# A second feed-forward stage by Strassen's seven products, in 256-token chunks, with ScalarE's mish and memory handed over by stage

## The chip, the cores and the metric

The kernel runs on one core of a Trainium2 chip. The metric is device time in microseconds of one execution. The engines are TensorE (PE; its weight loads appear as PEld), VectorE (DVE), ScalarE (ACT), GpSimd (POOL) and SyncE (SP), which issues all DMAs of this kernel.

## The reference

Attention with a memory term over 4 batches of 576 tokens, then two feed-forward stages over all 2304 tokens. The change is in the last one, `_moe2_ref`:

```
x = attention(q, k, v, M_prev, z_prev, beta)     # 2304 x 512
a = x @ w1; b = x @ w2; x = (a * b @ w3) @ w_out # first stage, 512 -> 1024 -> 512
h = x @ w_in                                     # second stage, 512 -> 2048
sp = where(h > 20, h, log1p(exp(min(h, 20))))
g = h * tanh(sp)                                 # mish
return g @ w_out                                 # 2048 -> 512
```

The weights come as float64. `conv` reads each as two 32-bit words and makes a float32 of it.

## The kernel before

The kernel records its operations and orders them itself. `Recorder.op` notes an operation with its engine, its estimated cost and the buffers that it reads and writes; `schedule` then simulates the engines with these costs and writes the instructions in the order that comes out. TensorE's operations keep nearly the order in which they were recorded (their key is their number plus a bias); the other engines take what is most urgent. A buffer is a tag with a fixed number of copies (`BUFS`), so an operation also waits until an older copy of its tag is free. Each engine executes its instructions strictly in the order written.

Products are made of float32 operands split into a high part (a cast to the format fp32r) and a low part (the rest): `HL` gives three matmuls, high x high, high x low and low x high, where one would do in lower precision. All matmuls are issued at line 331 (`mm`), whatever their stage.

The program has three parts. Attention (heads of `SC`, `SE`, `AV`) and the first feed-forward stage (`ffn1`, `ffn1o`) are interleaved; the first stage writes its result, transposed, to a DRAM tensor `x2d`. The last units of the first stage run alone after attention has ended. Then comes the second stage:

- `load_ffn2(m)` loads two 128-row weight blocks (512 KB each) and splits them into high and low parts. They go into memory that earlier parts have done with, by the list `HOMES` (tags V, QK, e0, ld, PH of attention; wE, wB, wD, wA of the first stage's weights; Rr, mnl). The raw data pass through three buffers (`RAWS`: Rr and two of mnl). Some of these loads are recorded among the last first-stage units (`F2N`).
- The tokens are cut into five chunks (`CH`: three of 512, two of 384). `load_x2` reads a chunk from `x2d` and splits it.
- `h_blk(c, m)`, for each of 16 blocks of 128 hidden features: 12 matmuls as wide as the chunk (4 parts of the model dimension x 3), then mish by hand: Exp, two VectorE operations, Ln, Exp, two VectorE multiplications, and the split of the result into `gh` and `gl`.
- `fin(c, m, ...)`, four blocks later (`LA`=4): for each 128-token part of the chunk three matmuls 512 wide, accumulated over the 16 blocks in a PSUM bank of its own.
- At the chunk's end ScalarE copies each bank out, and SyncE writes it.

PSUM has eight banks (tag g) for everything. The accumulators of a 512 chunk take four.

Of the kernel before, what the change touches and what calls it, by code (L numbers as in the profile page):

```python
# [14 lines left out]
P = 128  # L15
NEG = -8.0e9
E20 = 485165195.40979028
# [55 lines left out]
class Recorder:  # L73
# [9 lines left out]
    def op(self, eng, cost, fn, r=(), w=()):  # L83
# [26 lines left out]
        return o  # L110

# [152 lines left out]
def kernel(  # L264
# [40 lines left out]
    const = ctx.enter_context(tc.tile_pool(name="const", bufs=1))  # L305
    wp = ctx.enter_context(tc.tile_pool(name="wp", bufs=1))
    sp_ = ctx.enter_context(tc.tile_pool(name="sp", bufs=1))
# [19 lines left out]
    def dma(dst, src, nbytes, r=(), w=()):  # L327
        op("sp", max(500, nbytes / 340.0), lambda: nc.sync.dma_start(out=dst(), in_=src()), r, w)
# [20 lines left out]

    mask = const.tile([P, P], BF16, name="mask")  # L350
# [4 lines left out]
    two = const.tile([P, 1], F32, name="two")  # L355
# [7 lines left out]
    nc.vector.memset(two, 2.0)  # L363
# [310 lines left out]
    def conv(src, rawb, c=None, part=None):  # L674
# [9 lines left out]
        act(512, cv, lambda: hw().bitcast(F32), [(raw, 1)], [ck], False, AF.Prelu, scale=2.0 ** -111, alpha=-(2.0 ** 32))  # L684
# [13 lines left out]
    def wcol(t, h, kk):  # L698
        return t.tile[:, h].rearrange("p (k f) -> p k f", k=KD)[:, kk, :]
# [89 lines left out]
    wi, wt = {}, {}  # L789
    HOMES = ["V", "QK", "QK", "e0", "ld", "PH"] + ["wE"] * 4 + ["wB"] * 8 + ["wD"] * 4 + ["wA"] * 8 + ["Rr", "mnl"]  # L790
    RAWS = ("Rr", "mnl", "mnl")

    def load_ffn2(m):
        for n, dst, src in ((2 * m, wi, moe2_w_in), (2 * m + 1, wt, moe2_w_out)):
            load_w(dst, src, m, HOMES[n], lambda n=n: buf(RAWS[n % 3 if n < 30 else 2], [P, 512, 2], I32))

    CH = [(sum(CFG["CH"][:x]), n) for x, n in enumerate(CFG["CH"])]
    xc = {}

    def load_x2(c):  # L800
        t0, n = CH[c]
        need = [x for x in range(2 * B) if x * HS < t0 + n and (x + 1) * HS > t0]
        xc[c] = []
        for kk in range(KD):
            raw = buf(("vr", "pl")[kk % 2], [P, 512])
            dma(lambda kk=kk, raw=raw: raw.tile[:, 0:n], lambda kk=kk: x2d[kk * P:(kk + 1) * P, t0:t0 + n], 512 * n,
                r=[(fx2[x], 2 * (kk // 2) + 1) for x in need], w=[raw])
            xx = buf("u", [P, 2, 512], F32R)
            act(n, lambda raw=raw, xx=xx: xx.tile[:, 0, 0:n], lambda raw=raw: raw.tile[:, 0:n], [raw], [(xx, 0)])
            lo(n, lambda raw=raw, xx=xx: xx.tile[:, 1, 0:n], lambda raw=raw: raw.tile[:, 0:n], lambda xx=xx: xx.tile[:, 0, 0:n], [raw, (xx, 0)], [(xx, 1)])  # L810
            xc[c].append(xx)

    def h_blk(c, m):
        n = CH[c][1]
        ps = gbuf()
        for kk in range(KD):
            def f(kk=kk):
                for y, (wx, x) in enumerate(HL):
                    mm(ps.tile[:, 0:n], wcol(wi[m], wx, kk), xc[c][kk].tile[:, x, 0:n], kk == y == 0, kk == KD - 1 and y == 2)

            op("pe", 3 * t_mm(n), f, r=[(wi[m], 0), (wi[m], 1), (xc[c][kk], 0), (xc[c][kk], 1)], w=[ps])
        hv = lambda: ps.tile[:, 0:n]
        ub_ = buf("x", [P, 512])
        wb = buf("x", [P, 512])
        gh = buf("x", [P, 512], F32R)
        gl = buf("t", [P, 512], F32R)
        u = lambda: ub_.tile[:, 0:n]
        w_ = lambda: wb.tile[:, 0:n]
        act(n, u, hv, [ps], [ub_], True, AF.Exp, scale=2.0 ** -8)
        op("dve", t_dve(n, True), lambda: nc.vector.tensor_scalar(out=w_(), in0=u(), scalar1=E20, scalar2=2.0, op0=ALU.min, op1=ALU.add), r=[ub_], w=[wb])  # L830
        op("dve", t_dve(n), lambda: nc.vector.scalar_tensor_tensor(out=u(), in0=u(), scalar=E20, in1=w_(), op0=ALU.min, op1=ALU.mult), r=[ub_, wb], w=[ub_])  # L831
        act(n, w_, u, [ub_], [wb], False, AF.Ln, bias=two)
        act(n, w_, w_, [wb], [wb], False, AF.Exp, scale=-1.0)
        op("dve", t_dve(n), lambda: nc.vector.scalar_tensor_tensor(out=u(), in0=hv(), scalar=2.0 ** -8, in1=u(), op0=ALU.mult, op1=ALU.mult), r=[ps, ub_], w=[ub_])  # L834
# [5 lines left out]
    def fin(c, m, gt, acc):  # L840
        gh, gl = gt
        for t in range(CH[c][1] // P):
            ts_ = slice(t * P, (t + 1) * P)

            def f(ts_=ts_, t=t):
                o = acc[t][1]()
                mm(o, gh.tile[:, ts_], wt[m].tile[:, 0], m == 0, False)
                mm(o, gh.tile[:, ts_], wt[m].tile[:, 1], False, False)
                mm(o, gl.tile[:, ts_], wt[m].tile[:, 0], False, m == M2 - 1)

            op("pe", 3 * t_mm(512), f, r=[gh, gl, (wt[m], 0), (wt[m], 1)], w=[acc[t][0]])
# [113 lines left out]
    m2 = 0  # L965
    for n, u in enumerate(units[ui:]):
        u()
        if n >= CFG["F2N"][0] and n % CFG["F2N"][1] == 0 and m2 < CFG["F2N"][2]:
            load_ffn2(m2)
            m2 += 1  # L970
    load_x2(0)
    for m in range(m2, M2):
        load_ffn2(m)
    for c in range(len(CH)):
        t0, n = CH[c]
        acc = []
# [71 lines left out]
```

## Time and profile before

| | |
|---|---|
| median of 3 runs | 963.48 us (961.24 to 964.03) |
| the profiled execution | 963.81 us, its span 962.0 us |
| PE busy | 942.1 us (98%), 5440 matmul records |
| VectorE busy | 727.4 us (76%) |
| ScalarE busy | 607.4 us (63%) |
| GpSimd busy | 84.1 us (9%) |
| granted clock of PE | 0.996 of full over the span |
| chain that ended last | PE 73%, VectorE 14%, ScalarE 5%, DMA 3% |

The span runs from the first instruction of the program to its last; what lies around it is the 1.8 us between the two numbers. Times in the rows below count from the span's start. A matmul's end is modelled in these profiles, so the distance from one start to the next is what tells its cost.

### The profile page before, as it was taken

Reading aid. Unit: us, or ns where it says so; the run is one execution under the profiler, and the core shown is the slowest. Engines: PE = TensorE matmul, PEld = TensorE weight load, DVE = VectorE, ACT = ScalarE, POOL = GpSimd, SP = SyncE. Lnnn points to the kernel's source line nnn. Section 1 sums busy time; section 2 is a strip of 40 time slices with the busy share of each in tenths; the row PEclk is TensorE's granted clock in tenths of the full one; section 3 lists DMA queues with packets and bytes.
Section 4 is the critical chain, followed back from the end, with each engine's and each line's share of the span. In section 5 each row is a group of like instructions: output and inputs, shape, how many; then the busy total and the mean of one; then the engine's idle time right before and its main releaser. Section 6 shows DMA issues by size and latency. Waiting matters only on the chain.

```text
span 962.0 us, 15244 instructions
## 1 busy us (share of the span) xinstructions
PE 942.1 (98%) x5440; PEld 816.2 (85%) x5440; DVE 727.4 (76%) x1643; ACT 607.4 (63%) x1240; POOL 84.1 (9%) x70
## 2 busy tenths in 40 slices
PE   6999999999999999999999999999999999999998
PEld 3555888889899999999999988888888888998997
DVE  8999998899998889977573888537564756565663
ACT  6677776888787868766454676446454545554653
POOL 2111012312121102111000000000000000000000
PEclk9999999999999999999999999999999999999999
DMA  9779546434333424212572740020002000100000
GB/s 353 235 249 303 191 145 173 145 105 143 111 91 107 133 69 120 70 39 51 138 249 82 219 159 1 1 88 0 1 1 83 1 1 25 53 1 17 34 1 33
DMA packets 48316, 96.62 MB, mean 100 GB/s; under 512 B 11024, under 2 KB 23344, under 8 KB 48240
## 3 DMA queue, kind: packets, MB, share of 16 engines
q1 hardware_dynamic: 48240, 95.64, 31.9%
q8 instruction: 43, 0.70, 0.3%
q14 instruction: 33, 0.27, 0.1%
HBM read 85.85 MB, written 9.77 MB: 99 GB/s over the span
## 4 chain that ended last, share of the span: by engine, by line
PE 73%; DVE 14%; ACT 5%; DMA 3%; issue 3%; SPq 0%; POOL 0%; DVEq 0%; ACTq 0%; POOLq 0%
PE g L331 73%; DVE QK L334 2%; DVE t L348 2%; DVE e L348 1%; DVE mnl L348 1%; DVE t L687 1%; ACT t L340 1%; DVE wD L687 1%; DVE u L334 1%; DMA wA<-in_moe_w_out_dram 1%; ACT QK L338 1%; DVE g L561 1%; DMA vr<-x2d 1%; DVE u L685 1%; DVE e L334 1%
## 5 line engine op out<-in xcount | busy, mean ns | idle before, releaser
L331 PE MATMUL g<-u,wA 128*128 128x288 f32 (+2 forms) x1008 | 164.1, 315 | 1.5 <-DVE e L348 0.8
L331 PEld LDWEIGHTS g<-u,wA 128*128 128x128 f32 x1008 | 147.6, 188 | 10.1 <-DVE e L348 1.0
L348 DVE TENSOR_TENSOR t<-g,t 128x288 f32<-128x288 f32 (+6 forms) x344 | 121.8, 383 | 17.0 <-PE g L331 9.2
L581 POOL PARTITION_ALL_REDUCE t<-t x64 | 83.5, 1311 | 365.9 <-DVE t L348 323.1
L331 PE MATMUL g<-x,wB 128*128 128x288 f32 x768 | 111.7, 298 | 0.0
L331 PEld LDWEIGHTS g<-x,wB 128*128 128x128 f32 x768 | 105.0, 188 | 0.9 <-DVE e L348 0.2
L340 ACT ACTIVATE x<-x,two 128x512 f32<-128x512 f32 (+1 forms) x80 | 54.3, 681 | 68.0 <-DVE x L831 68.0
L340 ACT ACTIVATE x<-g 128x512 f32<-128x512 f32 (+1 forms) x98 | 54.7, 561 | 61.8 <-PE g L331 60.4
L331 PE MATMUL g<-e,V 128*65 128x320 f32 (+12 forms) x576 | 89.8, 302 | 1.8 <-DVE e L334 0.8
L331 PE MATMUL g<-QK 128*128 128x320 f32 (+7 forms) x464 | 77.1, 305 | 6.7 <-DVE QK L334 5.8
L834 DVE SCALAR_TENSOR_TENSOR x<-g,x 128x512 f32<-128x512 f32 (+1 forms) x80 | 50.9, 637 | 42.2 <-ACT x L340 41.8
L331 PEld LDWEIGHTS g<-e,V 128*65 128x65 f32 (+1 forms) x576 | 66.8, 137 | 18.6 <-ACT e L340 2.1
L338 ACT CAST x<-x 128x512 fp32r<-128x512 f32 (+1 forms) x80 | 46.1, 577 | 52.6 <-DVE x L348 52.5
L331 PEld LDWEIGHTS g<-QK 128*128 128x128 f32 x464 | 66.8, 196 | 14.6 <-DVE QK L334 8.0
L830 DVE TENSOR_SCALAR x<-x 128x512 f32<-128x512 f32 (+1 forms) x80 | 31.7, 398 | 59.7 <-ACT x L340 58.0
L334 DVE TENSOR_TENSOR t<-x 128x512 fp32r<-128x512 f32 (+1 forms) x80 | 50.9, 637 | 32.3 <-ACT x L338 31.1
L331 PE MATMUL g<-wB,wD 128*128 128x512 f32 x128 | 61.1, 617 | 3.7 <-DVE wD L687 2.1
L334 DVE TENSOR_TENSOR QK<-ld,QK 64x640 fp32r<-64x640 f32 (+1 forms) x80 | 59.7, 747 | 3.7 <-ACT QK L338 2.4
L331 PE MATMUL g<-x,wD 128*128 128x288 f32 x384 | 56.9, 297 | 0.3 <-DVE e L348 0.3
L331 PE MATMUL g<-x,wE 128*128 128x288 f32 x384 | 55.1, 299 | 0.6 <-ACT mnl L338 0.6
L348 DVE TENSOR_TENSOR x<-x 128x512 f32<-128x512 f32 (+1 forms) x80 | 51.0, 638 | 6.1
L831 DVE SCALAR_TENSOR_TENSOR x<-x 128x512 f32<-128x512 f32 (+1 forms) x80 | 50.9, 637 | 4.6
(147 smaller groups left out, 1810.1 us busy)
## 6 DMA issues: line engine op xcount, KB each, us to landing
ld<-in_qk_dram SPq DMA_DIRECT2D x24, 608.0 KB
u<-in_moe_w_dram SPq DMA_DIRECT2D x26, 512.0 KB
Rr<-d SPq DMA_DIRECT2D x24, 288.0 KB
mnl<-in_moe_w_out_dram SPq DMA_DIRECT2D x11, 512.0 KB
mnl<-in_moe_w_in_dram SPq DMA_DIRECT2D x11, 512.0 KB
x2d<-t SPq DMA_DIRECT2D x16, 288.0 KB
out_dram<-x SPq DMA_DIRECT2D x18, 256.0 KB
wA<-in_moe_w_out_dram SPq DMA_DIRECT2D x8, 512.0 KB
```

Of the source, the lines that this page charges most:

```text
L331: nc.tensor.matmul(out=o, lhsT=lhsT, rhs=rhs, start=start, stop=stop)
L334: eng.tensor_tensor(out=o, in0=a, in1=b, op=ALU.subtract)
L338: op("act", t_act(n, psum), lambda: nc.scalar.copy(out=o(), in_=i()), r, w)
L340: op("act", t_act(n, psum), lambda: nc.scalar.activation(out=o(), in_=i(), func=func, **kw), r, w)
L348: op(eng, t_dve(n) if eng == "dve" else t_pool(n), lambda: e.tensor_tensor(out=o(), in0=a(), in1=b(), op=alu), r, w)
L561: nc.vector.tensor_tensor(out=o, in0=o, in1=mv, op=ALU.add)
L581: op("pool", 430 + 2.6 * (b - a), lambda mv=mv: nc.gpsimd.partition_all_reduce(mv(), mv(), P, bass_isa.ReduceOp.max), r=[(m, x)], w=[(m, x)])
L685: op("dve", t_dve(512, True), lambda: nc.vector.tensor_scalar(out=lw(), in0=lw(), scalar1=29, scalar2=None, op0=ALU.logical_shift_right), ...
L687: op("dve", t_dve(512), lambda: nc.vector.scalar_tensor_tensor(out=ci(), in0=ci(), scalar=3, in1=lw(), op0=ALU.logical_shift_left, op1=ALU ...
L830: op("dve", t_dve(n, True), lambda: nc.vector.tensor_scalar(out=w_(), in0=u(), scalar1=E20, scalar2=2.0, op0=ALU.min, op1=ALU.add), r=[ub_ ...
L831: op("dve", t_dve(n), lambda: nc.vector.scalar_tensor_tensor(out=u(), in0=u(), scalar=E20, in1=w_(), op0=ALU.min, op1=ALU.mult), r=[ub_, w ...
L834: op("dve", t_dve(n), lambda: nc.vector.scalar_tensor_tensor(out=u(), in0=hv(), scalar=2.0 ** -8, in1=u(), op0=ALU.mult, op1=ALU.mult), r= ...
```

## The change

The second stage is written anew, and the memory around it.

- **Chunks** are 256 tokens (nine of them). The hidden features are taken in eight pairs of 128-blocks. `h_blk` makes both blocks of a pair in the two halves of one PSUM bank: 24 matmuls 256 wide.
- **Mish** is one ScalarE activation over the 512 columns of that bank (`AF.Mish`). It needs another table of functions; a recorded entry `table` puts its load after all uses of the old one.
- **The output product** treats two 128-token halves by two 128-feature halves as a 2 x 2 matrix, the output weights (two feature halves by two halves of 256 output columns) likewise, and multiplies them by Strassen's method (Winograd's form): seven products where there were eight. `g_blk` makes the sums on the token side for each pair (VectorE: operations of 128, 256 and 128 columns), then the split over 7 x 128 = 896 columns. `combine` makes the sums on the weight side, once, in chunk 0: four subtractions of 256 columns and splits of 1024 and 768. `fin` multiplies: seven products of three matmuls, 256 wide, each added into one of seven PSUM half-banks (`PRODUCTS`). `out_blk` puts the output together from them, by one ScalarE and four VectorE operations, and two writes of 256 KB.
- **Look-ahead** is two pairs (`LA`=2, before four blocks).
- **Memory** is handed over by stage. Two stacks of pools (`Room`): A1 holds what attention uses and becomes A2 (converted weights f, raw buffers s) when attention has ended; R1 holds what the first stage uses (x, u, t) and becomes R2 (G, H, ob, m) when that has ended. A tile of the new room waits for the tiles of the old one that lay where it lies. All 32 weight loads are therefore recorded after attention, through four raw buffers. Three pairs of input weights are loaded only when splits of earlier ones have given up their f buffers.

The diff, cut to its core:

```diff
+class Room:
+    def open(self):
+        if self.before is not None:
+            self.before.pool.release()
+        self.pool = self.tc.alloc_tile_pool(name=self.name, bufs=1, side=self.side, reuse_waits="tile")
...
+    def follow(self, room):
+        room.gate = o = self.op("pool", 0.0, room.open)
+        o.after = {x for x in self.ops if any(b.pool is room.before for b in x.bufs)}
...
+        "f": 13, "s": 4, "G": 2, "H": 2, "ob": 1, "m": 11, **CFG.get("BUFS", {}),
+    R1, A1 = Room(tc, "r1", "left"), Room(tc, "a1", "right")
+    R2, A2 = Room(tc, "r2", "left", R1), Room(tc, "a2", "right", A1)
...
+    def combine(i):
+        c, m = LC[i], buf("ob", [P, 3, 256])
+        for o, a, b in ((lambda: quarter(m, 0), lambda: quarter(c, 1), lambda: quarter(c, 3)),
+                        (lambda: quarter(c, 1), lambda: quarter(c, 1), lambda: quarter(c, 0)),
+                        (lambda: quarter(m, 1), lambda: quarter(c, 3), lambda: quarter(c, 1)),
+                        (lambda: quarter(m, 2), lambda: quarter(c, 2), lambda: quarter(m, 1))):
+            tt(256, o, a, b, ALU.subtract, [c, m], [c, m])
...
     def h_blk(c, m):
-        act(n, u, hv, [ps], [ub_], True, AF.Exp, scale=2.0 ** -8)
...
-        act(n, w_, u, [ub_], [wb], False, AF.Ln, bias=two)
-        act(n, w_, w_, [wb], [wb], False, AF.Exp, scale=-1.0)
...
+                            mm(ps.tile[:, y * CT:(y + 1) * CT], w[a].tile[:, y, kk * P:(kk + 1) * P], xc[c][j].tile[:, b, k * CT:(k + 1) * CT],
...
+    def g_blk(ps):
+        op("act", t_act(512, True), lambda: nc.scalar.activation(out=G.tile[:, 0:4].rearrange("p a b -> p (a b)"), in_=ps.tile, func=AF.Mish, scale=2.0 ** -8),
+           [ps, table], [(G, 0)])
+        tt(P, lambda: g(4), lambda: g(0), lambda: g(2), ALU.add, [(G, 0)], [(G, 1)])
+        tt(2 * P, lambda: G.tile[:, 5:7], lambda: G.tile[:, 0:5:4], lambda: g(1).unsqueeze(1).to_broadcast([P, 2, P]), ALU.subtract, [(G, 0), (G, 1)], [(G, 1)])
+        tt(P, lambda: g(7), lambda: g(3), lambda: g(6), ALU.subtract, [(G, 0), (G, 1)], [(G, 1)])
+        act(7 * P, lambda: H.tile[:, 0], g7, [(G, 0), (G, 1)], [(H, 0)])
+        lo(7 * P, lambda: H.tile[:, 1], g7, lambda: H.tile[:, 0], [(G, 0), (G, 1), (H, 0)], [(H, 1)])
...
+    PRODUCTS = [(0, 0, 0, 3, 0), (2, 0, 2, 0, 1), (5, 1, 1, 0, 0), (3, 0, 1, 1, 1), (4, 1, 0, 1, 0), (6, 0, 3, 2, 1), (1, 1, 2, 2, 0)]
+    def fin(c, i, H, acc):
+        for n, (k, d, qd, bank, half) in enumerate(PRODUCTS):
...
+                mm(o, gh, quarter(U, qd), i == 0 and first, False)
+                mm(o, gh, quarter(L, qd), False, False)
+                mm(o, gl, quarter(U, qd), False, i == NP2 - 1 and last)
...
+    rec.follow(A2)
+    loads = [(LC, moe2_w_out, i, y) for i in range(NP2) for y in range(2)]
+    loads += [(WC, moe2_w_in, i, y) for i in range(5) for y in range(2)]
     for n, u in enumerate(units[ui:]):
         u()
+        if n >= CFG["F2N"] and loads:
+            conv2(*loads.pop(0))
+    rec.follow(R2)
+    for i in range(NP2):
+        split_in(i)
+        if i < 3:
+            for y in range(2):
+                conv2(WC, moe2_w_in, i + 5, y)
+    op("act", 1400, lambda: None, w=[table])
+    load_x2(0)
+    for c in range(NC):
+        acc = [gbuf() for _ in range(4)]
...
+                if c == 0:
+                    combine(i)
+                ps = h_blk(c, i)
+            if i >= LA:
+                fin(c, i - LA, gts.pop(i - LA), acc)
+            if i < NP2:
+                gts[i] = g_blk(ps)
+            if i == NP2 - 1 and c + 1 < NC:
+                load_x2(c + 1)
+        out_blk(c, acc)
```

What this makes of the order of the instructions shows at three places. First TensorE, at the end of the first stage (the 96 matmuls of `ffn1o` with wA) and the begin of the second. Before:

```order
L331 MATMUL g<-u,wA 128x288 x96
L331 MATMUL g<-u,V 128x512 x3
L331 MATMUL g<-u,QK 128x512 x3
L331 MATMUL g<-u,V 128x512 x3
L331 MATMUL g<-u,QK 128x512 x3
L331 MATMUL g<-u,ld 128x512 x6
L331 MATMUL g<-u,wE 128x512 x9
```

And in the change (s is the chunk's data, wE and wB input weights; the rows with H are the output products, with weights of wA, f and m):

```order
L357 MATMUL g<-u,wA 128x288 x96
L357 MATMUL g<-s,wE 128x256 x48
L357 MATMUL g<-s,wB 128x256 x42
L357 MATMUL g<-wA,H 128x256
L357 MATMUL g<-f,H 128x256
L357 MATMUL g<-wA,H 128x256 x2
L357 MATMUL g<-f,H 128x256
L357 MATMUL g<-wA,H 128x256
L357 MATMUL g<-m,H 128x256 x3
L357 MATMUL g<-wA,H 128x256
L357 MATMUL g<-f,H 128x256
```

All of TensorE's order up to the 96 is the same; after it 90 matmuls 256 wide stand ahead of the first output product, where matmuls 512 wide stood.

Second VectorE, in the change, from the last of the four subtractions of the first `combine` on, where the second stage begins (before, its five mish operations per block stood here). ob, f and m belong to `combine`, G and H to `g_blk`:

```order
L374 TENSOR_TENSOR ob<-f,ob 128x256
L360 TENSOR_TENSOR f<-f,wA 128x1024
L374 TENSOR_TENSOR G<-G 128x128
L360 TENSOR_TENSOR m<-ob,m 128x768
L374 TENSOR_TENSOR G<-G 128x256
L374 TENSOR_TENSOR ob<-f 128x256
L374 TENSOR_TENSOR G<-G 128x128
L374 TENSOR_TENSOR f<-f 128x256
L374 TENSOR_TENSOR G<-G 128x128
L374 TENSOR_TENSOR ob<-f 128x256
L374 TENSOR_TENSOR G<-G 128x256
L360 TENSOR_TENSOR H<-G,H 128x896
```

The first residual of H (128x896), which the first output product needs, stands behind the rest of the first `combine` and half of the second.

Third SyncE, around the end of attention. The write and read of d and Rr belong to the last heads. Before:

```order
L328 DMA d_576_5861<-R 2x576 x2
L328 DMA cz<-d_576_5861 64x18
L328 DMA mnl<-in_moe_w_out_dram 128x1024
L328 DMA d_576_5861<-R 2x576
L328 DMA cp<-d_576_5861 128x18
L328 DMA mnl<-in_moe_w_in_dram 128x1024
L328 DMA d_576_6140<-cp 128x18
L328 DMA mnl<-in_moe_w_in_dram 128x1024
L328 DMA Rr<-d_576_6140 64x2x576 x2
L328 DMA x2d<-t 128x2x288
L328 DMA mnl<-in_moe_w_out_dram 128x1024
L328 DMA Rr<-in_moe_w_in_dram 128x1024
```

And in the change:

```order
L354 DMA cp<-d_576_5852 128x18
L354 DMA d_576_6123<-cp 128x18
L354 DMA Rr<-d_576_6123 64x2x576 x2
L354 DMA x2d<-t 128x2x288
L354 DMA s<-in_moe_w_out_dram 128x1024 x2
L354 DMA x2d<-t 128x2x288
L354 DMA s<-in_moe_w_out_dram 128x1024 x14
L354 DMA s<-in_moe_w_in_dram 128x1024 x7
L354 DMA x2d<-t 128x2x288
L354 DMA s<-in_moe_w_in_dram 128x1024 x3
L354 DMA x2d<-t 128x2x288
L354 DMA s<-in_moe_w_in_dram 128x1024 x6
```

The weight loads stood among the last heads' transfers and now stand behind them; two writes of x2d stand between the loads.

## Rows read from the trace of the kernel before

**Rows 1.** The page: busy time, share of the span and instructions of each engine.
```profile
PE 942.1 (98%) x5440; PEld 816.2 (85%) x5440; DVE 727.4 (76%) x1643; ACT 607.4 (63%) x1240; POOL 84.1 (9%) x70
```

**Rows 2.** Stretches of 50 us in the second stage; columns in the first line.
```profile
core 0: us, PE busy (x) PEld busy (x) DVE busy (x) ACT busy (x) POOL busy (x), PEclk, DMA share, GB/s
...
606.00:656.00 50.00, 50.00 (x216) 40.35 (x215) 25.93 (x43) 24.20 (x39) 0.00 (x0) 1.00 0.13 43
...
706.00:756.00 50.00, 50.00 (x216) 40.37 (x215) 29.55 (x48) 26.64 (x44) 0.00 (x0) 1.00 0.12 40
```

**Rows 3.** Chain that ended last, from 556 us on: shares by line.
```profile
by line: PE g L331 97.4%; DMA vr<-x2d 1.4%; DVE u L334 0.2%; ACT u L338 0.2%; ACT x L340 0.1%; issue 0.0%
```

**Rows 4.** PE in order: start us, us, engine, line, operation, tiles, shape, count.
```profile
543.34 12.86 PE L331 MATMUL g<-u,wA 128*128 128x288 f32 x96
556.04 0.87 PE L331 MATMUL g<-u,V 128*128 128x512 f32 x3
...
584.64 2.95 PE L331 MATMUL g<-u,wB 128*128 128x512 f32 x12
...
590.21 2.96 PE L331 MATMUL g<-u,wB 128*128 128x512 f32 x12
...
849.68 2.25 PE L331 MATMUL g<-u,wB 128*128 128x384 f32 x12
851.76 0.62 PE L331 MATMUL g<-wE,x 128*128 128x512 f32 x2
...
957.90 0.39 PE L331 MATMUL g<-mnl,t 128*128 128x512 f32 x1
```

**Rows 5.** PE in order, short matmuls of an attention head and what follows.
```profile
444.15 1.93 PE L331 MATMUL g<-QK 128*128 128x256 f32 x14
445.92 2.44 PE L331 MATMUL g<-e,V 128*65 128x256 f32 x21
448.20 4.96 PE L331 MATMUL g<-x,wB 128*128 128x288 f32 x36
```

**Rows 6.** The page: weight loads, count | busy us, mean ns | idle before.
```profile
L331 PEld LDWEIGHTS g<-x,wB 128*128 128x128 f32 x768 | 105.0, 188 | 0.9 <-DVE e L348 0.2
```

**Rows 7.** VectorE in order, at attention's end and in the second stage.
```profile
476.96 1.36 DVE L348 TENSOR_TENSOR mnl<-mnl,Rr 128x1152 f32<-128x1152 f32 x1
478.24 0.69 DVE L334 TENSOR_TENSOR ld<-t,ld 128x512 fp32r<-128x512 f32 x1
...
480.15 0.83 DVE L334 TENSOR_TENSOR x<-mnl,x 128x288 fp32r<-128x288 f32 x2 [0.55 <-ACT x L338]
...
659.08 0.69 DVE L348 TENSOR_TENSOR x<-x 128x512 f32<-128x512 f32 x1
659.69 0.69 DVE L831 SCALAR_TENSOR_TENSOR x<-x 128x512 f32<-128x512 f32 x1
```

**Rows 8.** ScalarE's groups, 640 to 760 us: count | busy us, mean ns | idle.
```profile
L340 ACT ACTIVATE x<-g 128x512 f32<-128x512 f32 x30 | 17.8, 593 | 25.4 <-PE g L331 24.9
L340 ACT ACTIVATE x<-x,two 128x512 f32<-128x512 f32 x22 | 15.9, 723 | 20.1 <-DVE x L831 20.1
...
L338 ACT CAST x<-x 128x512 fp32r<-128x512 f32 x22 | 13.6, 619 | 15.0 <-DVE x L348 15.0
```

**Rows 9.** ScalarE in order: a table load, and a copy from PSUM.
```profile
0.72 1.28 ACT L359 ACT_TABLE_LOAD   x1 [0.72 <-PEq L1008]
...
557.07 0.38 ACT L338 COPY t<-g 128x288 f32<-128x288 f32 x1
```

**Rows 10.** SyncE's issues of weight loads in order.
```profile
457.32 0.36 SPq L328 DMA_DIRECT2D mnl<-in_moe_w_out_dram  x1
...
490.13 0.33 SPq L328 DMA_DIRECT2D mnl<-in_moe_w_out_dram  x1
...
503.15 0.33 SPq L328 DMA_DIRECT2D mnl<-in_moe_w_out_dram  x1
```

**Rows 11.** Who waited for whom on SyncE, 940 to 962 us: total, times, longest.
```profile
SPq L1043 <- DMA out_dram<-x: 1.7, 1, 1.7
```

More of the change, by code (lines that the diff above doesn't have):

```diff
@@ L93, in op @@
                         o.after.add(b.users[0])
+                    elif isinstance(b.pool, Room) and b.pool.gate:
+                        o.after.add(b.pool.gate)
                     b.users.append(o)
@@ L669, in AV, with conv @@
             lo(HS, lambda u=u: u.tile[:, 1, :], lambda c=c: mnl.tile[:, 1, c], lambda u=u: u.tile[:, 0, :], [mnl, (u, 0)], [(u, 1)])
-    def conv(src, rawb, c=None, part=None):
+    def conv(src, rawb, c=None, part=None, *more):
         raw = rawb()
@@ L786, in ffn1o @@
                 r=[(o, 0), (o, 1)], w=[(fx2[2 * b + hf], dp)])
[L789 to L797, printed above, removed]
@@ L800, in load_x2 @@
     def load_x2(c):
-        t0, n = CH[c]
-        need = [x for x in range(2 * B) if x * HS < t0 + n and (x + 1) * HS > t0]
+        t0 = c * CT
+        need = [x for x in range(2 * B) if x * HS < t0 + CT and (x + 1) * HS > t0]
         xc[c] = []
[L804 to L810, printed above, removed]
+        raw = buf("s", [P, 2, 2 * CT])
@@ L840, in fin @@
[L840 to L851, printed above, removed]
+        w = (WH[i], WL[i])
@@ new lines, in out_blk, with add @@
+    def out_blk(c, acc):
+        ob = buf("ob", [P, 4, DH])
+        o = lambda a, b=None, s=1: ob.tile[:, a:b:s] if b else ob.tile[:, a]
+        pair = lambda k: acc[k].tile.rearrange("p (a b) -> p a b", b=DH)
+        sc = 2.0 ** -8
+        def add(n, dst, ps, other, r, w):
+            op("dve", t_dve(n), lambda: nc.vector.scalar_tensor_tensor(out=dst(), in0=ps(), scalar=sc, in1=other(), op0=ALU.mult, op1=ALU.add), r=r, w=w)
+        wide = lambda k: o(k).unsqueeze(1).to_broadcast([P, 2, DH])
+        act(DH, lambda: o(0), lambda: acc[3].tile[:, 0:DH], [acc[3]], [ob], True, AF.Identity, scale=sc)
+        add(512, lambda: o(1, 3), lambda: pair(0), lambda: wide(0), [acc[0], ob], [ob])
+        add(512, lambda: o(0, 4, 3), lambda: pair(1), lambda: wide(1), [acc[1], ob], [ob])
+        add(DH, lambda: o(1), lambda: acc[1].tile[:, DH:512], lambda: o(0), [acc[1], ob], [ob])
+        add(512, lambda: o(0, 4, 3), lambda: pair(2), lambda: o(0, 4, 3), [acc[2], ob], [ob])
+        for t in range(2):
+            r0 = c * CT + t * P
+            dma(lambda r0=r0: out[r0:r0 + P, :], lambda t=t: ob.tile[:, 2 * t:2 * t + 2].rearrange("p a b -> p (a b)"), 262144, r=[ob])
```

132 lines of the change are left out of this document (76 added, 56 removed), and 1 row of the table BUFS.

## The prediction

> **What bounds the kernel now.** I read the page first, then the stretches after the first feed-forward stage, the chain of waits there, and last the timeline of each engine. The page says that TensorE (PE) is busy for 98% of the span [rows 1]. A busy PE need not be a fast one, so the stretches must say whether anything holds it up: from 606 us on, PE is busy for all 50 us of a stretch at granted clock 1.00, while VectorE has 26 to 30 us of work and ScalarE 24 to 27 [rows 2]. The chain that ended last gives 97.4% of the time from 556 us to matmuls [rows 3]. So the second stage costs what its matmuls cost one after another, and ScalarE and VectorE have room. Relieving those two is worth nothing by itself; only fewer or cheaper matmuls, the two ends of the stage, or a new wait can move the time.
>
> The stage begins at 556.04 us and its last matmul starts at 957.90 [rows 4]. With 0.23 us for that one, it takes **402.1 us**.
>
> **What a matmul costs.** Their ends are modelled, so I take start to start within long runs of one width [rows 4]. Width 288: 96 in 556.04 - 543.34 = 12.70 us, 132.3 ns each. Width 384: 12 in 851.76 - 849.68 = 2.08 us, 173.3 ns. Width 512: a block of 12 and its 12 output matmuls from 584.64 to 590.21, 232.1 ns. Check: 1440 of 512 and 384 of 384 give 334.2 + 66.5 = 400.7, and the stage took 402.1.
>
> **The change, part by part.**
>
> *Matmuls.* The stage had 5 x 16 blocks of 12 (960) and 16 x 18 x 3 output matmuls (864): 1824. It gets 9 chunks x 8 pairs x (24 + 21) = 3240, all 256 wide. The 24 are the same columns cut finer; the 21 (7 products x 3) replace what would be 24. So columns fall from 884,736 to 829,440, by 6.3%, but each matmul has a part that does not shrink with its width. No long run of width 256 exists before. Going down from 288 by the slope between 288 and 384 (0.427 ns a column) gives 132.3 - 13.7 = 118.6 ns; by the mean slope from 288 to 512 (0.446), 118.0. Shrinking 288 in proportion, with no fixed part, gives 117.6 and is the bound below. The bound above is the 288 pitch itself, 132.3, since a narrower matmul should not cost more. The line fits three widths, so I take 118.6: 3240 x 0.1186 = 384.3 us, **17.8 us less**. A nanosecond of pitch is 3.2 us.
>
> What could keep the pitch off the line is that each matmul loads its own weights, and there are 1416 more loads. The shortest runs show what the loading path can do [rows 5]: 21 pairs of load and matmul with 64 or 65 weight columns went in 448.20 - 445.92 = 2.28 us, 108.6 ns each. With full 128-column weights, 14 of widths 64 to 320 (229 on average) took 1.77 us, 126.4 ns, because the narrowest of them could not go below their load. The load rows themselves read 188 ns, but 768 of them, 144 us, cover 105.0 us [rows 6], so they overlap one another, and at 288 they keep up at 132.3.
>
> The Trainium skill (Perfetto Trace Analysis, Identifying the Most-Contended Engine) says to judge the room left on TensorE by the summed time of the weight loads, and speaks against this change. By it, 3240 loads of 188 ns would make the stage 609 us, some 207 longer than before. The trace disagrees: the 188 ns rows follow each other at 132.3 ns.
>
> *Element work, later chunks.* Per pair, four ScalarE passes and five VectorE operations over 512 columns become one ScalarE pass from PSUM (Mish) and a cast of 896 columns, and VectorE operations of 128, 256, 128 and 896. The like ScalarE pass takes 0.593 us, the cast 0.619 for 512 [rows 8]; for 896, by 0.83 ns a column, 0.94. VectorE's pitch is 1.28 us for 1152 columns and 0.61 for 512 [rows 7], 1.047 ns a column and 0.07 fixed: 128 takes 0.21, 256 0.34, 896 1.01, and the four 1.77. Against 45 x 0.1186 = 5.34 us of matmuls per pair both are far off the path: cost 0. Mish has no row; between 0.593 and three passes like the dearest that it replaces (3 x 0.723 = 2.2 us [rows 8]) it stays hidden. It is hidden by the look-ahead of two pairs, some 10 us.
>
> *Chunk 0.* There VectorE also combines the output weights, once: 4 x 0.34 + 1.15 (1024 columns) + 0.88 (768) = 3.39 us more, 5.16 us per pair against 5.34. That is nearly even: no loss by the sum, and if its chained operations wait for each other at 0.5 us a pair, 0.3 x 8 = 2.6 us late. I take 1.1.
>
> *The first output product.* PE can run 90 matmuls before it needs one, until 556.04 + 10.7 = 566.7. The scratch of the combination lies where the first stage's output copies lay, so it waits for the last one's write. The last matmul of the first stage ends near 556.3; its copy takes 0.38 [rows 9], its write 2.0 (as the last output write now: 0.33 to issue [rows 10], then a wait of 1.7 [rows 11]): 558.9 with the hand-overs. Then come, in VectorE's order, four chained subtractions (1.9), ScalarE's copy of 1024 (1.1), the 1024 residual (1.15), the wait for the table load and Mish (0.8), then 768 (0.88), five of 256 (1.7), three of 128 (0.6), and the residual of H (1.1): 9.2 us, until 568.1. **PE waits 1.4 us**. Bounds: 0 if the write lands at once, 4 if each step hands over 0.2 us late.
>
> *Loading.* The first weight of this stage is issued at 457.32 us now [rows 10], and in the change only after attention's last use of its memory: VectorE's last write of x starts at 480.15 [rows 7]. 32 loads remain for 76 us. Now six intervals of the three-buffer ring (seven issues) take 503.15 - 490.13 = 13.0 us, 2.17 each [rows 10], 6.5 us per buffer; with four buffers that is 1.63 each, and 26 loads end at 522. The last 6 follow when the first stage gives up its weights, around 524 to 535, 20 us before use. SP also holds the writes of x2d among these loads, but no load waits for one that is itself late. Cost 0; at 2.17 per load it is 480 + 69 = 549, still before 556, though ScalarE stands in order and every load that is late holds up the first stage's copies behind it. I keep 0 to 5 us. The table load (1.28 us [rows 9]) waits for the last conversion and lies under the 90 matmuls.
>
> *Chunk ends and tail.* The next chunk's first two blocks are put ahead of the last products, and eight PSUM banks leave four free: cost 0. At the end, 957.90 + 0.23 to 962.0 is 3.9 us: a PSUM pass, the last issue, the landing. Now a VectorE pass of 512 (0.69) takes ScalarE's place and two writes leave together: **0.4 to 1.2 more, I take 0.7**.
>
> Sum: -17.8 + 1.4 + 1.1 + 0.7 = -14.6. The profiled execution took 963.8, so **949.2**. That execution is 0.3 over the median of the runs, below what a measurement tells apart (0.3%, 2.9 us), so I say 949.
>
> **Rivals.**
>
> *Weight loads set the pitch (slower).* With 256 columns the margin between a matmul and the next load is thin, and the 14-run at 126.4 ns shows that loads can win. For it: that run is the only one here with 128-column weights and a mean width under 256. Against it: its widths of 64 explain it, and 21 pairs ran at 108.6. The change turns into a loss where 3240 pitches plus 3.2 us pass 402.1: above 123.1 ns. At 126.4 the stage is 409.5, the time 963.8 + 7.4 + 3.2 = 974; at 132.3 it is 993. Chance 0.10, of which 0.02 lies near no change.
>
> The Trainium skill (TensorE: Matmul & The Clock Gate, Wait — 56ns, not 53.3ns?) gives about 62 ns per MATMUL where the sequencer decodes in firmware. If a load cost as much, a pair would be 124 ns, the stage 401.8 and the time, by estimate, 967. The 108.6 ns pairs of [rows 5] speak against it, though over 21 pairs only.
>
> *Late hand-over.* Everything is right, but the conversions, now squeezed in behind attention, hold up the first stage or start the second one late. For it: 27 us less time to load, and a ring that filled every 2.17 us. Against it: one buffer more and 20 us to spare. Price 5 to 8: 954 to 957. Chance 0.17.
>
> *No gain.* The products are fewer, but small losses at every chunk border add up: nine borders of 1.5 us would give back 13.5 and end at 963. Against it: at today's borders PE waits for nothing [rows 2]. Chance 0.03.
>
> **How the numbers follow.** The forecast has 0.70. Its own ends: 117.6 ns and no waits, 963.8 - 21.1 + 0.4 = 943; 120 ns and 5 us of waits, 963.8 - 13.3 + 6.2 = 957. The late hand-over lies inside, so 943 to 957 holds 0.85 or so. Faster: forecast and late hand-over, 0.87; within 0.3%: 0.05; slower: 0.08.
>
> **What would show it.** Right: from the second stage's start to its last matmul about 386 us, 45 matmuls in 5.34 us in the middle of a chunk, PE busy all through at clock 1.00, one wait of 1 to 3 us about 10 us into the stage, the stage starting at 556. Wrong: a pitch over 123 ns; VectorE as the releaser of many PE waits in the first 45 us of the stage; PE idle before 556 behind ScalarE's conversions; waits at each chunk's first products.

## The result and the profile after

The changed kernel took 950.39 us (median of 4 runs, 948.53 to 950.89) against 962.66 before: ratio 0.9869, 95% interval 0.9848 to 0.9890. A second measurement, the run r4_change_again, gave 0.9868 (0.9851 to 0.9885). The forecast was 949.

> The change once more, as the measure for the others on this chip: 950 (948.5 to 951).

The page of the changed kernel, engine line and three groups (columns as in [rows 1] and [rows 6]):

```profile
PE 925.6 (98%) x6856; PEld 863.8 (91%) x6856; DVE 686.2 (72%) x1588; ACT 529.7 (56%) x1046; POOL 85.2 (9%) x70
...
L360 DVE TENSOR_TENSOR H<-G,H 128x896 fp32r<-128x896 f32 x72 | 78.7, 1093 | 96.3 <-ACT H L364 96.2
...
L364 ACT CAST H<-G 128x896 fp32r<-128x896 f32 x72 | 67.9, 944 | 118.2 <-PE g L357 98.1
...
L890 ACT ACTIVATE G<-g 128x512 f32<-128x512 f32 x72 | 43.0, 597 | 95.0 <-PE g L357 87.6
```

TensorE is as busy as before in share, 98%, with 1416 more matmuls. Mish is one ScalarE pass of 597 ns.

Stretches of the second stage (columns of [rows 2]):

```profile
650.00:700.00 50.00, 50.00 (x422) 50.00 (x421) 24.75 (x47) 16.14 (x22) 0.00 (x0) 1.00 0.07 22
700.00:750.00 50.00, 50.00 (x423) 50.00 (x422) 23.26 (x44) 15.89 (x22) 0.00 (x0) 1.00 0.07 22
```

PE is busy for all 50 us at clock 1.00, as in [rows 2], with 422 matmuls where 216 stood. Now the weight loads fill the stretch as well (50.00; before 40.4). That says little by itself: rows of 188 ns, as in [rows 6], that start 119 ns apart must overlap. How much margin is left between a matmul and the next load is measured below (r8). TensorE in order in the middle of a chunk shows the pitch:

```profile
702.67 3.04 PE L357 MATMUL g<-s,wB 128*128 128x256 f32 x24
...
708.02 3.04 PE L357 MATMUL g<-s,wB 128*128 128x256 f32 x24
710.90 0.28 PE L357 MATMUL g<-wA,H 128*128 128x256 f32 x1
```

From one block's start to the next, 45 matmuls take 5.35 us, 119 ns each. A row of 24 holds 23 pitches and the last one's own 0.28: (3.04 - 0.28) / 23 = 120.0 ns for a hidden matmul. The 21 of the output take (713.38 - 710.90) / 21 = 118 ns; 713.38 is where the next block starts.

The start of the stage, TensorE, VectorE and ScalarE in order:

```profile
553.82 2.83 PE L357 MATMUL g<-u,wA 128*128 128x288 f32 x20
556.48 5.92 PE L357 MATMUL g<-s,wE 128*128 128x256 f32 x48
562.24 5.20 PE L357 MATMUL g<-s,wB 128*128 128x256 f32 x42
567.28 0.28 PE L357 MATMUL g<-wA,H 128*128 128x256 f32 x1
567.40 0.28 PE L357 MATMUL g<-f,H 128*128 128x256 f32 x1
568.13 0.51 PE L357 MATMUL g<-wA,H 128*128 128x256 f32 x2 [0.46 <-DVE H L360]
...
559.40 0.43 DVE L374 TENSOR_TENSOR ob<-f 128x256 f32<-128x256 f32 x1 [11.52 <-DMA x2d<-t]
...
560.78 0.42 DVE L374 TENSOR_TENSOR ob<-f,ob 128x256 f32<-128x256 f32 x1
561.40 1.23 DVE L360 TENSOR_TENSOR f<-f,wA 128x1024 fp32r<-128x1024 f32 x1 [0.20 <-ACT wA L364]
563.31 0.29 DVE L374 TENSOR_TENSOR G<-G 128x128 f32<-128x128 f32 x1 [0.69 <-ACT G L890]
564.03 0.96 DVE L360 TENSOR_TENSOR m<-ob,m 128x768 fp32r<-128x768 f32 x1 [0.43 <-ACT m L364]
...
566.99 1.09 DVE L360 TENSOR_TENSOR H<-G,H 128x896 fp32r<-128x896 f32 x1
...
560.32 1.05 ACT L364 CAST wA<-f 128x1024 fp32r<-128x1024 f32 x1 [3.23 <-DVE f L374]
561.38 1.28 ACT L890 ACT_TABLE_LOAD   x1
562.68 0.60 ACT L890 ACTIVATE G<-g 128x512 f32<-128x512 f32 x1
```

VectorE stands idle for 11.52 us until the last write of x2d has landed, because the combined weights go where the first stage's copies lay. From there to 568.08, the end of H's residual, it only pauses for ScalarE (0.20, 0.69 and 0.43 us). TensorE reaches that residual 0.46 us too early. That is its only wait in the stage that the records name; the starts show one more of 0.3 us at 572.7 (below). The table load lies under the 90 matmuls.

The loading, SyncE's queue in order, and the end of the kernel on TensorE, VectorE and that queue:

```profile
481.09 21.68 SPq L354 DMA_DIRECT2D s<-in_moe_w_out_dram  x14
503.75 10.60 SPq L354 DMA_DIRECT2D s<-in_moe_w_in_dram  x7
...
521.12 12.52 SPq L354 DMA_DIRECT2D s<-in_moe_w_in_dram  x6
534.28 9.49 SPq L354 DMA_DIRECT2D s<-x2d  x4
...
943.08 0.52 PE L357 MATMUL g<-f,H 128*128 128x256 f32 x3
...
942.27 2.74 DVE L925 SCALAR_TENSOR_TENSOR ob<-g,ob 128x512 f32<-128x512 f32 x4 [1.50 <-PE g L357]
...
945.09 0.81 SPq L354 DMA_DIRECT2D out_dram<-ob  x2
```

The last weight load is issued by 533.6, 23 us before the stage. At the end the four VectorE adds need 2.74 us and end 1.6 us after TensorE's last matmul (start 943.32, and 0.12 for its pitch).

### The profile page after: what moved, and what is told of

It is laid out like the page before. It is cut to its first block, busy times and chain, and to the rows that moved or that the text cites. A ratio compares the mean times of both kernels' runs of the same rounds, so it can differ in the third digit from the quotient of the medians.

```text
span 949.1 us, 17745 instructions
## 1 busy us (share of the span) xinstructions
PE 925.6 (98%) x6856; PEld 863.8 (91%) x6856; DVE 686.2 (72%) x1588; ACT 529.7 (56%) x1046; POOL 85.2 (9%) x70
## 4 chain that ended last, share of the span: by engine, by line
PE 68%; DVE 19%; ACT 5%; DMA 4%; issue 3%; POOL 1%; SPq 0%; DVEq 0%; ACTq 0%; POOLq 0%
PE g L357 68%; DVE t L374 4%; DVE QK L360 3%; DVE e L374 2%; DVE mnl L374 2%; DVE g L586 1%; DMA Rr<-d 1%; POOL t L606 1%; DMA d<-cp 1%; DVE e L360 1%; DVE u L360 1%; DVE wD L712 1%; DMA u<-in_moe_w_dram 1%; ACT QK L364 1%; ACT mnl L364 1%
## 5 line engine op out<-in xcount | busy, mean ns | idle before, releaser
L360 DVE TENSOR_TENSOR H<-G,H 128x896 fp32r<-128x896 f32 x72 | 78.7, 1093 | 96.3 <-ACT H L364 96.2
L357 PE MATMUL g<-wA,H 128*128 128x256 f32 x576 | 135.8, 281 | 0.5 <-DVE H L360 0.5
L374 DVE TENSOR_TENSOR G<-G 128x128 f32<-128x128 f32 (+1 forms) x216 | 72.5, 335 | 58.3 <-ACT G L890 53.8
L357 PE MATMUL g<-u,wA 128*128 128x288 f32 x768 | 110.9, 298 | 1.6 <-DVE e L374 0.8
L357 PE MATMUL g<-f,H 128*128 128x256 f32 x477 | 111.7, 280 | 0.0
L357 PE MATMUL g<-s,wB 128*128 128x256 f32 x864 | 109.5, 282 | 0.0
L357 PEld LDWEIGHTS g<-s,wB 128*128 128x128 f32 x864 | 106.1, 188 | 0.0
L357 PEld LDWEIGHTS g<-wA,H 128*128 128x128 f32 x576 | 103.0, 189 | 0.7 <-DVE H L360 0.7
L357 PEld LDWEIGHTS g<-e,V 128*65 128x65 f32 (+1 forms) x576 | 66.7, 137 | 20.1 <-ACT e L366 3.7
L357 PE MATMUL g<-m,H 128*128 128x256 f32 x459 | 83.3, 281 | 0.0
L357 PEld LDWEIGHTS g<-f,H 128*128 128x128 f32 x477 | 82.1, 188 | 0.0
```

The source lines that it names most:

```text
L357: nc.tensor.matmul(out=o, lhsT=lhsT, rhs=rhs, start=start, stop=stop)
L360: eng.tensor_tensor(out=o, in0=a, in1=b, op=ALU.subtract)
L374: op(eng, t_dve(n) if eng == "dve" else t_pool(n), lambda: e.tensor_tensor(out=o(), in0=a(), in1=b(), op=alu), r, w)
```

## The experiments

The first theory was the prediction's: the stage costs its matmuls, and the gain is the eighth product's matmuls less what finer cutting costs. The rivals were the relief of ScalarE and VectorE by Mish, the loading, and a floor set by the weight loads.

**Eight products (r1_eight).** The change without Strassen: the output block by the plain eight products, no combined weights, no sums of G.

```diff
-        for n, (k, d, qd, bank, half) in enumerate(PRODUCTS):
...
+        for t in range(2):
+            for half in range(2):
+                for y in range(2):
...
-        acc = [gbuf() for _ in range(4)]
+        acc = [gbuf() for _ in range(2)]
```

> The change with the plain product (eight products of 256 columns instead of seven, no sums on either side, no combination in chunk 0), all else as in the change: chunks, Mish, memory. Theory (the stage costs its matmuls): 3456 matmuls at the 118.3 ns that the changed kernel showed instead of 3240, 25.6 us more, less some 2 us for the lighter start and end: 972 to 975, slower than the kernel before. Rival (the gain came from Mish and the relief of ScalarE and VectorE, or from the memory): within 2 us of the changed kernel, 949 to 952.

Measured: 971.33 us, ratio to before 1.0094 (1.0079 to 1.0109): slower than the kernel before, as expected, and 0.7 below the expected range. All else in the change together makes the kernel 9 us slower. From its first to its last matmul the stage takes 410.8 us here and 386.8 in the change. Of the 216 x 0.119 = 25.7 us of matmuls that the seven products save, 24.0 arrive; 1.0 of the rest are late starts in the change's first chunk. Less the 1.9 of a longer end and the 2.0 that the stage started earlier in this run, that leaves 20.1 between the two profiles, and 20.9 between the two medians. The pitch is the same as in the change though VectorE works a third as much:

```profile
700.00:750.00 50.00, 50.00 (x423) 50.00 (x422) 7.32 (x11) 13.33 (x22) 0.00 (x0) 1.00 0.07 22
```

**Mish in the kernel before (r2_mish_only).** The new table is loaded after the last weight conversion (at 568.0 us).

```diff
-        act(n, u, hv, [ps], [ub_], True, AF.Exp, scale=2.0 ** -8)
...
+        op("act", t_act(n, True), lambda: nc.scalar.activation(out=u(), in_=hv(), func=AF.Mish, scale=2.0 ** -8), [ps, table], [ub_])
```

> The kernel before with one part of the change alone: Mish as one ScalarE pass in place of the three function passes and four VectorE operations. Theory (ScalarE and VectorE are hidden): nothing gained, 963; the load of the new table has to wait for the last weight conversion, which before ends some 10 us into the second stage, so up to 5 us may be lost there: 962 to 968. Rival (relieving them is part of the gain): 951 to 958.

Measured: 961.74, ratio 0.9991 (0.9978 to 1.0004): no difference. Relief of engines that are not the bound is worth nothing there. The 5 us that the table load could have cost did not show either.

**Chunks of 256 in the kernel before (r3_chunk256).**

```diff
-    CH=[512, 512, 512, 384, 384],
+    CH=[256] * 9,
```

> The kernel before with nine chunks of 256 tokens in place of 512, 512, 512, 384, 384, and nothing else: the hidden matmuls become 1728 of 256 columns, the output ones stay 864 of 512. Theory (each matmul has a fixed part): 1728 x 0.1183 = 204.4 us in place of 576 x 0.2321 + 384 x 0.1733 = 200.2, 4.2 us more: 966 to 968. Rival (narrow matmuls cost only their columns): 962 to 963. If borders of chunks cost something, four more of them show on top.

Measured: 960.23, ratio 0.9972 (0.9959 to 0.9984). A miss: it was to be slower and is faster. Its hidden matmuls are 256 wide, and no wait of TensorE's is on record, but the pitch is not 118.6 throughout. It goes with the tile of the weights:

```profile
690.56 1.59 PE L331 MATMUL g<-u,V 128*128 128x256 f32 x12
...
694.79 2.89 PE L331 MATMUL g<-u,wE 128*128 128x256 f32 x24
...
707.26 1.54 PE L331 MATMUL g<-u,wB 128*128 128x256 f32 x12
```

(1.59 - 0.28) / 11 = 119.1 ns with weights in V, (2.89 - 0.28) / 23 = 113.5 in wE, (1.54 - 0.28) / 11 = 114.5 in this wB; by the starts, 115.6 in the mean of all 1728. In the changed kernel it is 120.0, with the same width, the same two weights per product and clock 1.00. So width alone does not give the pitch. This opened the second question, taken up below.

**The change with mish by hand (r5_hand_mish).** The three ScalarE and four VectorE passes of before, with half of G as scratch.

```diff
-        op("act", t_act(512, True), lambda: nc.scalar.activation(out=G.tile[:, 0:4].rearrange("p a b -> p (a b)"), in_=ps.tile, func=AF.Mish, scale=2.0 ** -8),
-           [ps, table], [(G, 0)])
...
+        act(512, u, lambda: ps.tile, [ps], [g0], True, AF.Exp, scale=2.0 ** -8)
...
+        act(512, w_, u, [g0], [g1], False, AF.Ln, bias=two)
+        act(512, w_, w_, [g1], [g1], False, AF.Exp, scale=-1.0)
```

> The change with the mish of before, by hand (three function passes on ScalarE, four operations on VectorE over 512 columns), and no second table. Theory (VectorE is hidden in the later chunks and nearly even in chunk 0): in later chunks VectorE has 1.77 + 2.1 = 3.9 us per pair against 5.32 of matmuls, no loss; in chunk 0 it has 7.3, so it falls behind by some 2 us a pair: 12 to 16 us in all, 962 to 966, with VectorE as the releaser of PE in the first 60 us of the stage only. Rival one (hidden everywhere): 950 to 952. Rival two (it costs in every chunk): over 975.

Measured: 961.44, ratio 0.9995 (0.9981 to 1.0010): all of the gain is gone. This is 0.6 below the expected range, and by luck so near it: the loss is larger than the 12 to 16 us forecast, and a second effect (r9 below) hides a part. Stretches of this run (columns of [rows 2]):

```profile
588.00:594.00 6.00, 4.72 (x39) 4.33 (x38) 6.00 (x13) 3.54 (x6) 0.00 (x0) 1.00 0.28 90
594.00:600.00 6.00, 4.13 (x32) 3.60 (x31) 6.00 (x10) 3.53 (x5) 0.00 (x0) 1.00 0.00 0
600.00:606.00 6.00, 3.71 (x30) 3.32 (x29) 5.49 (x12) 4.25 (x6) 0.00 (x0) 1.00 0.00 0
606.00:611.00 5.00, 5.00 (x32) 5.00 (x31) 4.96 (x12) 1.34 (x2) 0.00 (x0) 0.66 0.00 0
...
620.00:626.00 6.00, 5.61 (x34) 5.62 (x35) 6.00 (x13) 3.57 (x7) 0.00 (x0) 0.72 0.00 1
626.00:632.00 6.00, 6.00 (x53) 6.00 (x52) 5.24 (x11) 2.81 (x5) 0.00 (x0) 1.00 0.24 89
```

Most of the loss is in the first chunk: VectorE is busy for all of 588 to 600 (combined weights and mish together), TensorE waits for it or for ScalarE behind it (10.4 us between 570 and 625), and after the pauses the granted clock falls to 0.66, 32 matmuls in 5 us. From 626 to 945 us TensorE does not wait; at the very end, with no hidden matmuls left to cover mish, it waits another 1.9 us. The weights of this run were moved as in r9 below, so the nearest comparison is that run: 961.44 against 941.48, 20 us for mish by hand, of which the stage shows 18.9 (398.6 for 379.6). So Mish is worth nothing in the kernel before, and in the change it is what leaves room for the combination.

**A ring of three (r6_ring3).**

```diff
-        "f": 13, "s": 4, "G": 2, "H": 2, "ob": 1, "m": 11, **CFG.get("BUFS", {}),
+        "f": 13, "s": 3, "G": 2, "H": 2, "ob": 1, "m": 11, **CFG.get("BUFS", {}),
```

> The change with three raw buffers for the weights instead of four. Theory (the hand-over has room): a buffer's round of 6.5 to 7 us gives 2.2 to 2.3 us per load, the last loads end near 550 instead of 534, and at most 3 us are lost: 950 to 954. Rival (the loads are the edge, and late conversions hold up the first stage's copies on ScalarE): 955 to 965, with PE waiting before the second stage begins.

Measured: 949.73, ratio 0.9875 (0.9857 to 0.9893): no loss. SyncE's queue in order:

```profile
519.18 23.60 SPq L354 DMA_DIRECT2D s<-in_moe_w_in_dram  x11
543.96 0.89 SPq L354 DMA_DIRECT2D s<-x2d  x2
```

The last weight load is issued 9 us later than with four buffers, at 542.8, and there is still room: the stage starts at 553.9. The hand-over does not bind.

**The end (r7_tail).** In the last two pairs the products of banks 0, 1 and 3 go first, and the last add and the writes are cut by token half.

```diff
+                elif i - LA == NP2 - 1:
+                    for banks in ((0, 1, 3), (2,)):
+                        for k in (NP2 - 2, NP2 - 1):
+                            fin(c, k, gts[k], acc, banks)
```

> The change with a shorter end: in the last chunk the products of the last two pairs go first to the half-banks that the output sums need first, and the last sum and the two writes are cut by token half. Theory (the 5.7 us from the last matmul to the end are a chain of three VectorE operations, two writes and their landing): 0.7 to 1.4 us less from the last matmul to the end, 949 to 950. Rival (the writes alone set it): no change.

Measured: 949.34, ratio 0.9870 (0.9853 to 0.9886), not distinguishable from the change. The last matmul starts at 942.08 and the span ends at 947.6: 5.5 us instead of 5.8. That is less than the 0.7 to 1.4 expected. The adds still take 2.81 us in a row and end 1.6 us after the last matmul, so only 0.3 is won.

**Narrower hidden matmuls (r8_narrow192).** 22 of the 24 hidden matmuls of a pair are 192 wide. It leaves out part of the hidden sums: 64 of each 256 columns get only the first of their twelve parts.

```diff
+    HW = 192
...
-                            mm(ps.tile[:, y * CT:(y + 1) * CT], w[a].tile[:, y, kk * P:(kk + 1) * P], xc[c][j].tile[:, b, k * CT:(k + 1) * CT],
+                            n = CT if kk == z == 0 else HW
+                            mm(ps.tile[:, y * CT:y * CT + n], w[a].tile[:, y, kk * P:(kk + 1) * P], xc[c][j].tile[:, b, k * CT:k * CT + n],
```

> The change with 22 of the 24 hidden matmuls of each pair reading only 192 of their 256 columns (the last 64 columns of each half get only the first of their twelve parts): a measurement of what loading the weights allows. Theory (a load of 128 weight columns cannot be repeated faster than the 108 to 110 ns that the shortest distances between loads show): these matmuls go from 118.3 to about 109 ns, 1584 x 9.3 = 14.7 us less: 934 to 938. Rival (the cost goes on falling by 0.43 ns a column, to 91): 1584 x 27.5 = 43.6 us less, 905 to 910.

Measured: 936.86, ratio 0.9738 (0.9719 to 0.9758). TensorE in order (the row names the widest shape):

```profile
701.84 2.84 PE L357 MATMUL g<-s,wB 128*128 128x256 f32 x24
704.51 0.30 PE L357 MATMUL g<-wA,H 128*128 128x256 f32 x1
```

24 take 704.51 - 701.84 = 2.67 us, 111 ns with the two wide ones. A quarter fewer columns cost 7% less (2.88 us at 120.0 ns), not 25%. The weight loads explain it: in this run most loads for hidden matmuls start 111 or 112 ns after the one before, and in the run of 14 in [rows 5], also with 128 weight columns, loads beside the matmuls of 64, 128 and 192 columns start 108 or 111 ns apart, whatever the width. So with fresh weights of 128 columns the pitch hardly goes below 110 ns in these kernels. The 108.6 of the 21 pairs in [rows 5] is no such floor: it is a mean over matmuls of 64 to 320 columns with 64 or 65 weight columns, and single distances there go down to 30 ns.

**The place of the tiles (r9, r10, r11).** The hand-written mish run had some short hidden rows too (2.89 us for 24), and one tile of 4 bytes per partition ahead of the weights. By the programs' memory plans this shifts the weight tiles from multiples of 64 bytes to 32 past one, where the kernel before has them; the x2 tiles are 32 past one in all of these. No row of a trace shows an address, so these places rest on the plans alone. The three runs move tiles, with one short memset for each tile put in. Other tiles move with them: ob, G, m and H with the weights, the landing tiles with x2.

```diff
+    pad = wp.tile([P, 1], F32, name="pad")
...
+        if c == 0:
+            pd = buf("pd", [P, 8])
+            op("dve", 60, lambda: nc.vector.memset(pd.tile, 0.0), w=[pd])
```

The first line is r9_pad_weights, the other three r10_pad_moving, all of them r11_pad_both.

> The change with a tile of 4 bytes per partition put ahead of the weight tiles, and nothing else: the weight tiles and every tile that follows on their side (ob, G, m, H) now start 32 bytes past a multiple of 64 instead of at one; the x2 tiles stay at 32 past. This is also the only thing that the hand-written mish run had that could bear on a hidden product, and there one took 117.0 ns instead of 120.0, and one of the output 117.9 instead of 118.7. If the place of the weights in memory decides (or whether weights and moving data lie alike), 1728 hidden matmuls give back 3.0 ns and 1512 of the output 0.8: 5.2 + 1.2 = 6.4 us, so 943 to 945 us, with a hidden pitch near 117. If it is something else (the Mish instruction, the load on VectorE and ScalarE), the time stays at 949 to 951 and the pitch at 119 to 120.

> The change with a tile of 32 bytes per partition put behind the s tiles (x2, cast and residual, and the landing tiles of the weight loads), which moves them 32 bytes down to multiples of 64; weights stay at multiples of 64. If what counts is that weights and moving data lie alike, the hidden pitch falls to about 117 and the time by 1728 x 3.0 ns = 5 us, to 944 to 946. If what counts is the place of the weights alone, or neither, the time stays at 949 to 951.

> Both shifts together: weights 32 bytes past a multiple of 64, x2 tiles at multiples of 64. If the place of the weights alone counts, 943 to 945 us as with the first shift alone; if alike counts, back to 949 to 951 us for the hidden products (pitch near 120); if neither, 949 to 951.

TensorE in order, r9, then r10, then r11:

```profile
708.11 2.89 PE L357 MATMUL g<-s,wD 128*128 128x256 f32 x24
...
729.15 2.99 PE L357 MATMUL g<-s,wB 128*128 128x256 f32 x24
```

```profile
705.56 2.99 PE L357 MATMUL g<-s,wB 128*128 128x256 f32 x24
```

```profile
704.71 3.00 PE L357 MATMUL g<-s,wB 128*128 128x256 f32 x24
```

| run | weights, past a multiple of 64 | x2 tiles | 24 hidden matmuls | pitch | us | ratio to before |
|---|---|---|---|---|---|---|
| the change, again | 0 | 32 | 3.04 us | 120.0 | 949.66 | 0.9868 (0.9851 to 0.9885) |
| r9 | 32 | 32 | 2.89 (five pairs), 2.99 (three) | 113.5, 117.8 | 941.48 | 0.9788 (0.9773 to 0.9803) |
| r10 | 0 | 0 | 2.99 | 117.8 | 946.39 | 0.9842 (0.9819 to 0.9864) |
| r11 | 32 | 0 | 3.00 (2.96 in three pairs) | 118.3, 116.5 | 946.59 | 0.9836 (0.9820 to 0.9851) |

The first shift gives 8 us more, at the same mean clock of 0.998; 6.4 were expected. Its stage, from first to last start, takes 379.6 us instead of 386.8. By the starts, the 1728 hidden matmuls take 199.6 us instead of 207.4, and the output's 1512 take 0.6 more (180.1 for 179.5): together the 7.2 measured. The other 2.7 us of this profile is the stage before, which ended earlier. That end lies between 553.8 and 557.1 over all runs, whatever was changed, so I count 7 us as shown. Neither theory holds whole: "alike" predicts 120 for r11, "the weights alone" predicts 120 for r10, and both are near 118. So moving tiles by 32 bytes changes the pitch; which of the moved tiles counts, and by what mechanism, no run tells. The remainder by 64 is not the whole rule either: in r9 all weights lie alike by it, and three of the eight pairs stay at 117.8.

**Both (r12_pad_weights_tail).** The first shift and the edit of the end.

> The first shift (weights 32 bytes past a multiple of 64) and the tail edit together, as the version that should beat both kernels. With the first shift alone the median was 941.5 us, and the tail edit made the stretch from the last matmul to the end of the span 5.5 us long instead of 5.8: 941.2 us, between 940.3 and 942.2. If the 8 to 9 us of the first shift were a chance of that program's layout that any other edit undoes, the time would go back towards 949.

Measured: 943.25, ratio 0.9801 (0.9784 to 0.9818), 1 us above the expected range. The stage takes 379.6 us again, so the gain of the shift survives another edit of the program. The end's edit adds nothing that can be told. Both kernels with the first shift beat the kernel before by 2%, and the change by 0.7 to 0.8%.

## Why the prediction was right

| term | predicted, us | measured in the profiled execution |
|---|---|---|
| start of the stage | 556.04, unchanged | 556.48: +0.4 (553.8 to 557.1 over all runs) |
| matmuls, against 402.1 | 3240 x 118.6 ns: -17.8 | 3240 x 119.1 ns = 385.9: -16.2 |
| first product, chunk 0 | +1.4, +1.1 | +0.7, +0.3 (late starts) |
| tail | +0.7 | 5.7 for 3.9: +1.8 |
| sum | -14.6: 949.2 | -13.0: 950.8; the execution took 950.9 |

The number is nearer than the terms: the matmuls gained 1.6 us less than forecast and the end cost 1.1 more, while the waits cost 1.5 less.

- **What bounds.** Right. The chain of waits gives 369 us to one stretch of matmuls, and r2 shows that relief elsewhere is worth nothing:

```profile
568.13 4.81 PE g L357 x38
572.95 369.24 PE g L357 x3098
```

- **The pitch.** Right in size, 119.1 for 118.6, but for a weaker reason than I gave. The line through three widths is not a law for 256: the same width ran at 113.5 to 120.0 in these kernels, and the line's value lies between. r9's 113.5 is also below the 117.6 that I called the bound below. The error I allowed for was on the right scale; its cause was not in the text. The trace of before had a nearer price than the line: the attention heads hold 112 single matmuls of 256 columns (48 of them with 128 weight columns), and by the starts the distance to the next is 118 ns in the median.
- **The rival that weight loads set the pitch.** It fell: the stage stayed below the 123.1 ns at which it would lose. r8 shows that the rival has a real limit behind it, near 110 ns, only 9 ns below what the change runs at. One argument against it was misread: the 21 pairs at 108.6 ns load 64 or 65 weight columns for matmuls of 64 to 320, so they say nothing of a load of 128 columns. The two estimates that I made from the Trainium skill fail here. By the Trainium skill (Perfetto Trace Analysis, Identifying the Most-Contended Engine), loads of 188 ns would have made 609 us; the stage took 387. By the Trainium skill (TensorE: Matmul & The Clock Gate, Wait — 56ns, not 53.3ns?), its firmware figure would make 124 ns a pair on my assumption that a load costs as much; pairs ran at 113.5 to 120.0, and at 111 when narrower.
- **The first output product.** VectorE's chain was right in its parts, and to the tenth by luck: H's residual ends at 568.08, predicted 568.1, but the chain began 0.5 us later than I had it (559.40 for 558.9) and was 0.5 shorter (8.7 for 9.2). ScalarE's cast of 1024 ran at 560.32, beside the last two subtractions, where I had put it behind them. TensorE came 0.6 us later than predicted (567.28 for 566.7) and could run two matmuls on the cast half first, so a wait of 0.46 is left of the 1.4. By the starts, it and the slow start behind it cost 0.7.
- **Chunk 0.** I allowed 1.1 for VectorE being nearly even with TensorE. It cost 0.3: one group of three matmuls with the combined weights m takes 0.79 us where the others take 0.52, for VectorE's residual of m ends only at 572.89.

```profile
572.66 0.79 PE L357 MATMUL g<-m,H 128*128 128x256 f32 x3
...
571.94 0.95 DVE L360 TENSOR_TENSOR m<-ob,m 128x768 fp32r<-128x768 f32 x1
```

  r5 shows that the margin is real but thin: four passes more per pair, and TensorE waits.
- **The rival of losses at the borders.** It fell: after 573.2 us no two matmuls of the change start more than 128 ns apart, at borders of chunks or elsewhere.
- **Loading.** Right: 26 loads by 522 and six more until 535 predicted; the last six are issued from 521.1 to 533.6. r6 shows room for 9 us more.
- **The tail.** This is the term that was mis-sized: 1.8 us lies outside the 0.4 to 1.2 that I gave. I counted one VectorE pass of 512 after the last product; in fact the four adds begin when bank 0 is complete, take 2.74 us where TensorE's remaining products take 1.2, and end 1.6 us late.

## What to carry to other kernels

Where TensorE is full, count its instructions first, and give each a price from the trace at its own width; a cut into smaller matmuls must save more instructions than its pitch loses (here eight products lose 9 us and seven win 12). A change that adds element work needs the passes that hide it counted in its worst stretch, the first chunk here, not in the mean. When two kernels run the same matmul at different pitches, compare where the tiles lie: one shift by 32 bytes was worth 7 us here.

## What the runs showed of the hardware

- The pitch of a 128x128 by 256 matmul with fresh weights changed when tiles were moved by 32 bytes in a partition: 120.0 ns in the change, 113.5 and 117.8 in r9, 117.8 in r10, 118.3 and 116.5 in r11, at granted clock 1.00.
- Such a matmul hardly goes below 110 ns here: 24 of which 22 had 192 columns instead of 256 took 111 in the mean (r8), and in [rows 5] loads of 128 weight columns beside narrow matmuls start 108 or 111 ns apart.
- After pauses the granted clock fell: in the run with mish by hand TensorE had 30 matmuls in 600 to 606 us, with waits of 1.36 and 0.93 us, and in 606 to 611 it was granted 0.66, a mixture of the two levels. Part of the matmuls there came every 213 ns, which for 256 columns is the pace of 1.2 GHz, and again (0.72) in 620 to 626; from 626 on it stayed at 1.00. The 0.46 us wait of the change was followed by no such stretch.
